# Closing the tile context behind the first three loads, and clearing the semaphores while the last store is under way

## The chip, the cores and the metric

The kernel runs on one core of a Trainium2 chip. A core has five engines that run on their own and meet only through semaphores: PE (matmuls), DVE and ACT (elementwise work and reductions), POOL (here: fills) and SP (here: DMA issues). Sixteen DMA engines move data between HBM and the core's SBUF. The metric is the device time of one execution in microseconds (us). Each kernel is run several times; the median counts.

## The reference

One decode step for two batch entries `b`. Attention over a cache of 32768 positions with 32 query heads on 4 key-value heads, and an MLP mixer on the same `x`, are mixed by a gate:

```python
def reference(A_x, A_k_cache, A_v_cache, A_wq, A_wo, B_x, B_w1, B_w2, B_w3, B_w4, gate_w):
    x = A_x                                            # (2, 1, 1024)
    g = _sigmoid((x * gate_w).sum(-1, keepdims=True))
    q = (x @ A_wq).reshape(2, 1, 32, 128).transpose(0, 2, 1, 3)
    k, v = (jnp.repeat(c, 8, axis=1) for c in (A_k_cache, A_v_cache))   # (2, 4, 32768, 128) each
    p = _softmax(jnp.einsum("bhqd,bhkd->bhqk", q, k) * 128 ** -0.5, axis=-1)
    a = jnp.einsum("bhqk,bhkd->bhqd", p, v).transpose(0, 2, 1, 3).reshape(2, 1, 4096) @ A_wo
    # with one position in the sequence, every shift of the token mixing shifts in zeros: x1 = x
    b = x + _gelu(_layernorm(x) @ B_w3) @ B_w4
    return g * a + (1 - g) * b
```

All arrays are float32. The caches hold 2 x 4 x 32768 x 128 values each, 134 MB, and the kernel reads 331 MB from HBM for an output of 8 KB.

## The kernel before, in words

**Loads.** Two large buffers in SBUF, `load0` and `load1` (the list `ring`, 64 KB in each of 128 partitions), take all large arrays in turn. SP issues every such load through the helper `load` (line 208): it waits until the buffer's last readers are through, then issues the DMA, which adds 16 to a semaphore when it has landed. In order: two halves of `wq` (lines 238 and 239, no wait), two of `w3`, then for each of 8 pairs of batch entry and key-value head two halves of `kt` (the transposed keys) and two of `vt`, with two pieces of `w4` after the fourth pair, and at the end `wo` in four pieces to the ring and four small ones to the buffer `tail`. `xg`, which holds `x` and the gate's weights, is loaded by ACT (line 269, tile `xg_sb`).

**Compute.** While the first loads are in flight, POOL fills the padded operands with zeros (`wide`, `x_pad` to `w_pad`, lines 270 to 276) and DVE makes selection matrices (`sel`, `perm`, lines 279 to 293). When `xg_sb` has landed, DVE and PE make the norm and the gate; PE projects `x` by `wq` (`project`, line 350, matmuls in line 347) and the normed `x` by `w3`. Eight turns follow, one per pair: scores (line 463), exponentials on ACT (line 530), transposes (line 480) and the product with the values (line 489). `weigh` adds the products with `w4` and `wo`. The last pieces of `wo`, in `tail`, are multiplied behind that in two halves (line 370); ACT copies either half out of PSUM (line 612), SP stores the first and ACT the second (line 613).

**Order.** Nothing is scheduled: every engine has a list of instructions in the order of the code, and waits for semaphores that the code counts by hand (`Line.after` is a wait, `Line.take` a wait that also subtracts). All of it stands in one section of the tile framework, `tile_critical` (line 191), whose `sync_engine` is POOL. The framework puts three things around that: a meeting of all engines at the very start (each engine adds to a semaphore behind a drain, POOL waits for four, and releases them); at the section's start a NOP on POOL that the others wait for; at its end a drain on each engine, which POOL gathers, and then, behind ACT's own wait for the two stores (`stored`, line 615), a meeting of all engines, POOL's clear of the semaphores in one instruction, and a second meeting. Instructions of the framework carry the lines 640, 643 and 191 in the profile.

Of the kernel before, what the change touches and what calls it, by code (L numbers as in the profile page):

```python
# [9 lines left out]
F32 = mybir.dt.float32  # L10
# [4 lines left out]
P = 128  # L15
# [4 lines left out]
NI = 4  # L20
# [51 lines left out]
def kernel(  # L72
# [52 lines left out]
    nc = tc.nc  # L125
    scale = DH ** -0.5

    sb = ctx.enter_context(tc.tile_pool(name="sb", bufs=1))
    ps = ctx.enter_context(tc.tile_pool(name="ps", bufs=1, space=bass.MemoryType.PSUM))

    def new(name, *shape, parts=P):
        return sb.tile([parts, *shape], F32, name=name)

    ring = [new(f"load{i}", PART, WIDE) for i in range(2)]
    tail = new("tail", 4 * D)
    xg_sb = new("xg_sb", KD, 3)
    wide = new("wide", 3 * P)
    ones = new("ones", P)
# [38 lines left out]
    f = new("f", REP)  # L177
    so_far = new("so_far", D // G)
    out_sb = [new("out0", P), new("out1", P // 2)]

    sc = [ps.tile([P, 512], F32, name=f"sc{i}") for i in range(NI)]
    tr = [ps.tile([P, 512], F32, name=f"tr{i}") for i in range(2)]
    acc_bank = ps.tile([P, 512], F32, name="acc")
    acc = acc_bank[:, :D // G]
    final = [sc[0][:, :P], sc[1][:, :P // 2]]
    pv = ps.tile([P, 512], F32, name="pv")
    ident = wide[:, P:2 * P]
    compact = ident[:, ::C // B]

    section = ctx.enter_context(ExitStack())  # L190
    section.enter_context(tc.tile_critical(sync_engine=mybir.EngineType.Pool))
    sem = tc.alloc_semaphore
    pe, dve, act, pool = (Line(e, sem(n)) for e, n in (
        (nc.tensor, "pe"), (nc.vector, "dve"), (nc.scalar, "act"), (nc.gpsimd, "pool")))
    sp = Line(nc.sync)
# [1 line left out]
    landed = [sem(f"landed{i}") for i in range(2)]  # L197
    w_in = [*landed, sem("w_in2"), sem("w_in3")]
    got_x = sem("got_x")


    step, own_step, to_pe, pt_in, b_in, e_in, x_in, k1_free = (
        sem(n) for n in ("step", "own_step", "to_pe", "pt_in", "b_in", "e_in", "x_in", "k1_free"))

    came = ((got_x, 32), (b_in, 16), (pt_in, 16), (k1_free, PAIRS + 16))
    stored = x_in

    def load(dst, src, sem, *marks):
        sp.after(*marks)
        nc.sync.dma_start(dst, src).then_inc(sem, 16)  # L210

    def run(src, j):
        return src[PART * j:PART * (j + 1)].rearrange("i (q w) c -> (i q) (w c)", w=PART)

    flat = [t.rearrange("p w c -> p (w c)") for t in ring]
# [7 lines left out]
    def at(name, m=None):  # L223
        if m is None:
            return (pe.sem, 1 + PROLOGUE.index(name))
        return (pe.sem, len(PROLOGUE) + m * len(TURN) + m // 4 * 2 + 1 + TURN.index(name))
# [8 lines left out]

    load(flat[0], run(wq, 0), landed[0])
    load(flat[1], run(wq, 1), landed[1])
    load(flat[0][:, :PART * 2 * F], run(w3, 0), landed[0], at("q0"))  # L240
    load(flat[1][:, :PART * 2 * F], run(w3, 1), landed[1], at("q1"))

# [23 lines left out]
        load(tail[:, 3 * D + i * D // 2:3 * D + (i + 1) * D // 2], run(wo, 1)[:, lo:lo + D // 2], came[2 + i][0])  # L266


    nc.scalar.dma_start(xg_sb, xg).then_inc(got_x, 16)
    pool.mark(nc.gpsimd.memset(wide, 0.0))  # L270
    pool.after((pool.sem, pool.n))
    made = pool.mark(nc.gpsimd.affine_select(
# [325 lines left out]
    for mark, parts in zip(came, (((0, 0), (0, 1), (1, 0), (1, 1)), ((2, 0), (2, 1)), ((3, 0),), ((3, 1),))):  # L598
        pe.after(mark)
        for c, i in parts:  # L600
# [2 lines left out]
                             stop=(c == 3))  # L603
            if c == 3:
                last.then_inc(pe.sem, 1)
    thirty_two = nc.scalar.to_reg(32)

    to = [out.rearrange("(i k b) (h c) -> i h (k b) c", i=2, k=2, h=2)[0],
          out.rearrange("(i k b) (q h c) -> i h (k b q) c", i=2, k=2, q=2, h=2)[1]]
    for i, (line, step_of) in enumerate(((sp, 2 * SHIFT), (act, SHIFT))):  # L610
        act.after(ended(i))
        line.after(act.mark(nc.scalar.copy(out_sb[i], final[i])))  # L612
        line.e.dma_start(to[i], out_sb[i][::step_of]).then_inc(stored, 16)
    section.close()
    nc.scalar.nop(nofuse=True).wait_op(stored, thirty_two, "sem-ge")


# ---- launch: one core; the host only lays the arrays out
# [28 lines left out]
```

## Time and profile before

| | |
|---|---|
| time of the runs, median of 3 | 774.99 us (774.84 to 775.09) |
| span of the profiled execution | 773.0 us |
| PE busy | 434.3 us (56%) |
| DVE, ACT, POOL busy | 94.7, 60.8, 3.6 us |
| mean granted TensorE clock | 0.768 of full speed |
| read from HBM | 331.36 MB, 429 GB/s over the span |

The span of the profiled execution reaches from its first to its last instruction on any engine; the time of a run is longer, since it holds what lies around that. The page lists busy times of the engines without waits, branches, drains and DMA issues; such queue instructions are found by asking for a line of the code, and are marked with a "q" behind the engine's name (SPq, ACTq, POOLq; PEldq is PE's queue). For a DMA issue, the time in the list is that of the issuing instruction, not of the transfer.

### The profile page before, as it was taken

To read this page: it belongs to the slowest core of one execution; us is meant where nothing else is said; L and a number is where in the kernel's file an instruction comes from. 1 tells how busy PE (TensorE), PEld (TensorE's weight loads), DVE (VectorE), ACT (ScalarE), POOL (GpSimd) and SP (SyncE) were. 2 spreads that over 40 slices of the span, in tenths; PEclk is the share of its full clock that TensorE was granted. 3 is DMA by queue.
4 is the path that set the end of the run, shared out by engine and by line. 5 is a ranking of instruction groups with operands and counts; after the bars stand their busy time and mean duration, and the time that the engine had idled before them with its cause. 6 is when DMAs were issued, how large, how long until landed. Compare 5 with 4: busy or idle time off the path is not lost. (4 is left out here: it accounts for less than half of the span.)

```text
span 773.0 us, 7554 instructions
## 1 busy us (share of the span) xinstructions
PE 434.3 (56%) x3380; PEld 196.4 (25%) x3380; DVE 94.7 (12%) x267; ACT 60.8 (8%) x145; POOL 3.6 (0%) x12
## 2 busy tenths in 40 slices
PE   0576746564645474547475446454745465646466
PEld 0232413232322132223233213121312132313133
DVE  1110202100210021002100002100210021002110
ACT  0000002000200020002000002000200020002000
POOL 1000000000000000000000000000000000000000
PEclk9977667767887768766866779777777777779789
DMA  9999999999999999999999999999999999999997
GB/s 380 434 435 435 434 435 435 435 435 434 434 434 434 434 434 431 434 434 434 425 433 435 428 434 434 434 434 434 431 434 434 434 434 434 431 434 434 438 417 313
DMA packets 6805, 331.51 MB, mean 429 GB/s; under 512 B 900, under 2 KB 908, under 8 KB 1292
## 3 DMA queue, kind: packets, MB, share of 16 engines
q1 hardware_dynamic: 6634, 331.36, 99.2%
q8 instruction: 8, 0.13, 0.1%
q10 hardware_dynamic: 162, 0.02, 0.0%
q14 instruction: 1, 0.01, 0.0%
HBM read 331.36 MB, written 0.01 MB: 429 GB/s over the span
## 5 line engine op out<-in xcount | busy, mean ns | idle before, releaser
L463 PE MATMUL sc<-load,q_cur 128*32 128x512 f32 x1024 | 145.0, 727 | 133.1 <-PEq L51 133.1
L489 PE MATMUL pv<-load,pt 128*32 128x512 f32 x1024 | 132.0, 674 | 89.3 <-PEq L51 89.3
L463 PEld LDWEIGHTS sc<-load,q_cur 128*32 128x32 f32 x1024 | 48.0, 131 | 223.9 <-issue 223.0
L489 PEld LDWEIGHTS pv<-load,pt 128*32 128x32 f32 x1024 | 39.0, 123 | 172.3 <-issue 172.3
L480 PE MATMUL sc<-wide,p 128*128 128x128 f32 x256 | 44.4, 347 | 22.8 <-PEq L51 22.8
L546 DVE TENSOR_REDUCE mx<-sc 128x1 f32<-128x512 f32 x32 | 21.4, 689 | 286.4 <-PE sc L463 286.4
L530 ACT ACT_TABLE_LOAD x8 | 10.3, 1283 | 486.0 <-ACTq L51 486.0
L480 PEld LDWEIGHTS sc<-wide,p 128*128 128x128 f32 x256 | 40.0, 184 | 30.0 <-issue 30.0
L361 PE MATMUL acc<-load,w_pad 128*32 128x256 f32 x448 | 33.1, 465 | 18.1 <-PEq L51 18.1
L563 DVE COPY pt<-sc 64x256 f32<-64x256 f32 x64 | 25.9, 415 | 78.4 <-PE sc L480 77.9
L536 ACT COPY pt<-sc 64x256 f32<-64x256 f32 x64 | 23.5, 367 | 82.3 <-PE sc L480 80.0
L568 DVE COPY pv_sb<-pv 128x512 f32<-128x512 f32 x16 | 10.3, 686 | 146.8 <-PE tr L495 146.8
L361 PEld LDWEIGHTS acc<-load,w_pad 128*32 128x32 f32 x448 | 18.1, 133 | 32.4 <-issue 27.0
L499 PE MATMUL tr<-sel,pv_sb 128*128 128x8 f32 x128 | 19.0, 284 | 11.8 <-PEq L51 11.8
L347 PE MATMUL sc<-load,x_pad 128*32 128x512 f32 x128 | 18.6, 746 | 7.0 <-PEq L51 7.0
L499 PEld LDWEIGHTS tr<-sel,pv_sb 128*128 128x128 f32 x128 | 18.5, 230 | 12.3 <-issue 12.3
L530 ACT ACTIVATE p<-sc,bias 128x512 f32<-128x512 f32 x32 | 21.5, 685 | 0.1
L347 PE MATMUL sc<-load,xn_pad 128*32 128x384 f32 (+1 forms) x128 | 15.3, 640 | 7.9 <-PEq L51 7.9
L332 PE MATMUL tr<-xg_sb,perm 128*128 128x16 f32 x4 | 1.0, 372 | 23.1 <-DMA xg_sb<-xg 23.1
L559 DVE COPY p<-p 128x256 f32<-128x256 f32 x32 | 9.4, 294 | 26.7 <-ACT p L530 26.7
L347 PEld LDWEIGHTS sc<-load,x_pad 128*32 128x32 f32 x128 | 4.7, 133 | 20.0 <-issue 20.0
L347 PEld LDWEIGHTS sc<-load,xn_pad 128*32 128x32 f32 x128 | 4.8, 131 | 18.4 <-issue 18.4
(86 smaller groups left out, 96.5 us busy)
## 6 DMA issues: line engine op xcount, KB each, us to landing
load<-w SPq DMA_DIRECT2D x4, 7168.0 KB, 25.3
load<-wo SPq DMA_DIRECT2D x1, 7168.0 KB, 29.0
load<-wo SPq DMA_DIRECT2D x1, 4096.0 KB, 18.1
load<-wo SPq DMA_DIRECT2D x1, 2048.0 KB, 22.6
load<-wo SPq DMA_DIRECT2D x1, 1024.0 KB, 24.6
tail<-wo SPq DMA_DIRECT2D x1, 1024.0 KB, 26.6
tail<-wo SPq DMA_DIRECT2D x1, 512.0 KB, 27.4
tail<-wo SPq DMA_DIRECT2D x2, 256.0 KB, 27.6
```

Source lines behind the costliest of these rows:

```text
L347: last = nc.tensor.matmul(b[C * g:C * g + C, :hi - lo], pad[:, k], t[:, o + lo:o + hi], start=(k == 0), stop=(k == KD - 1))
L361: inst = nc.tensor.matmul(acc[C * g:C * g + C], lhsT, rows[:, g * (D // G):(g + 1) * (D // G)], start=False, stop=last, skip_group_check=True)
L463: last = nc.tensor.matmul(sc[i][C * g:C * g + C], q_cur[:, w, s], ring[j][:, w, o:o + 512], start=(s == 0 and w == 0), stop=(s == 1 and w ...
L480: last = nc.tensor.transpose(sc[k][:, t * P:(t + 1) * P], pair.rearrange("p w q -> p (w q)"), ident)
L489: last = nc.tensor.matmul(pv[C * g:C * g + C], pt[j][w][:, lo:lo + C], ring[j][:, w, o:o + G * DH], start=(j == 0 and w == 0 and t == 0), ...
L499: last = nc.tensor.matmul(tr[1][:, w * REP:(w + 1) * REP], pv_sb[:, s, w].rearrange("p i q -> p (i q)"), sel[:, s], start=(s == 0), stop=( ...
L530: nc.scalar.activation(p[:, i, :, :PART], sc[i].rearrange("p (t q w) -> p t w q", t=NT, w=PART), AF.Exp, bias=bias, scale=scale, accum_out ...
L536: nc.scalar.copy(*halves(1, j, c)).then_inc(pt_in, 1)
L546: last = [nc.vector.reduce_max(out=mx[:, k:k + 1], in_=sc[k], axis=AX.X) for k in ((1, 2) if i == 2 else (i,))][-1]
L559: nc.vector.tensor_copy(p[:, i, :, PART], p[:, i, :, 0]).then_inc(to_pe, 1)
L563: nc.vector.tensor_copy(*halves(0, j, c)).then_inc(pt_in, 1)
L568: last = nc.vector.tensor_copy(pv_sb[:, :, :, i], pv.rearrange("p (s q w) -> p s w q", q=HALF, w=PART))
```

## The change

SBUF and PSUM buffers are taken from the program directly in place of tile pools. The critical section now holds only the first two loads of `wq` and the load of `xg`, its `sync_engine` is SP, and the tile context is closed and compiled right behind it. All instructions after that are written straight to the engines. At the end no framework code is left: SP and ACT each add to a new semaphore `issued` behind their store, POOL waits for both and clears the kernel's semaphores (the list `cleared`, all but `stored`), and ACT's last instruction waits for the stores on `stored`, which has a semaphore of its own now and which ACT itself sets back.

```diff
-    sb = ctx.enter_context(tc.tile_pool(name="sb", bufs=1))
-    ps = ctx.enter_context(tc.tile_pool(name="ps", bufs=1, space=bass.MemoryType.PSUM))
-
     def new(name, *shape, parts=P):
-        return sb.tile([parts, *shape], F32, name=name)
+        return nc.alloc_sbuf_tensor(name, [parts, *shape], F32).ap()
+
+    def bank(name):
+        return nc.alloc_psum_tensor(name, [P, 512], F32).ap()
...
-    section = ctx.enter_context(ExitStack())
-    section.enter_context(tc.tile_critical(sync_engine=mybir.EngineType.Pool))
-    sem = tc.alloc_semaphore
+    cleared = []
+
+    def sem(name):
+        cleared.append(nc.alloc_semaphore(name))
+        return cleared[-1]
+
+    stored = nc.alloc_semaphore("stored")
...
+    issued = sem("issued")
...
-    stored = x_in
...
-    load(flat[0], run(wq, 0), landed[0])
-    load(flat[1], run(wq, 1), landed[1])
+    with tc.tile_critical(sync_engine=mybir.EngineType.SP):
+        for j in range(2):
+            load(flat[j], run(wq, j), landed[j])
+        nc.scalar.dma_start(xg_sb, xg).then_inc(got_x, 16)
+    tc.close()
+    tc.compile()
+
     load(flat[0][:, :PART * 2 * F], run(w3, 0), landed[0], at("q0"))
...
-    nc.scalar.dma_start(xg_sb, xg).then_inc(got_x, 16)
     pool.mark(nc.gpsimd.memset(wide, 0.0))
...
-    thirty_two = nc.scalar.to_reg(32)
...
         line.e.dma_start(to[i], out_sb[i][::step_of]).then_inc(stored, 16)
-    section.close()
-    nc.scalar.nop(nofuse=True).wait_op(stored, thirty_two, "sem-ge")
+        line.e.nop().then_inc(issued, 1)
+    nc.gpsimd.wait_ge(issued, 2)
+    nc.clear_and_free_semaphores(cleared)
+    act.take(stored, 32)
```

The change moves instructions at the two ends of each engine's list. The lists below name an instruction's line in its own kernel, what it writes and reads, and the semaphores that it waits for; plain increments, waits and drains are not listed. The start of SP's list, before (`Pool_sequencer` is the semaphore of POOL's NOP, the barrier is the meeting at the very start):

```order
L643 UNCONDITIONAL_BRANCH [waits barrier_Pool_Activation_PE_DVE_SP_release]
L643 UNCONDITIONAL_BRANCH [waits Pool_sequencer_49]
L210 DMA load_61<-wq 128x16384
L210 DMA load_62<-wq 128x16384
L210 DMA load_61<-w 128x14336 [waits pe]
```

and now:

```order
L652 UNCONDITIONAL_BRANCH [waits barrier_Pool_Activation_PE_DVE_SP_release]
L242 NO_OP
L247 UNCONDITIONAL_BRANCH [waits SP_sequencer_49]
L214 DMA load<-wq 128x16384 x2
L242 UNCONDITIONAL_BRANCH
L242 NO_OP [waits SP_49,SP_sequencer_49,Activation_sequencer_49]
L247 UNCONDITIONAL_BRANCH
L214 DMA load<-w 128x14336 [waits barrier_Pool_Activation_PE_DVE_SP_release,pe]
```

The NOP that lets the first loads go is now SP's own, and between the loads of `wq` and of `w3` stand the section's exit and the meetings of the context's end, which were the last thing in the program.

The end of POOL's list, before:

```order
L276 MEMSET w_pad 128x896
L210 UNCONDITIONAL_BRANCH
L191 UNCONDITIONAL_BRANCH
L191 NO_OP [waits Pool_49,DVE_sequencer_49,PE_sequencer_49,SP_sequencer_49,Activation_sequencer_49,Pool_sequencer_49]
L643 UNCONDITIONAL_BRANCH
L643 ISA [waits barrier_Pool_Activation_PE_DVE_SP_gather]
```

and now, with the context's end ahead of the fills:

```order
L652 UNCONDITIONAL_BRANCH [waits barrier_Pool_Activation_PE_DVE_SP_gather]
L247 UNCONDITIONAL_BRANCH x2
L247 ISA [waits barrier_Pool_Activation_PE_DVE_SP_gather]
L278 MEMSET wide 128x384 [waits barrier_Pool_Activation_PE_DVE_SP_gather]
...
L284 MEMSET w_pad 128x896
L623 ISA [waits issued]
```

The ISA rows are the clears. The one at the end no longer waits for a meeting of all engines, but for SP and ACT alone, and nothing follows it; a second, of the framework's own semaphores, stands near the start between two meetings that POOL, DVE, PE and ACT go through before their first instruction of the set-up.

The end of ACT's list, before:

```order
L612 COPY out_104<-sc_106 128x128 [waits pe]
L612 COPY out_105<-sc_107 128x64 [waits pe]
L613 DMA out<-out_105 2x8x64 [waits act]
L191 UNCONDITIONAL_BRANCH
L643 UNCONDITIONAL_BRANCH [waits Pool_49,x_in]
```

and now:

```order
L619 COPY out<-sc 128x128 [waits pe]
L619 COPY out<-sc 128x64 [waits pe]
L620 DMA out<-out 2x8x64 [waits act]
```

The two branches behind the store are gone; the increment of `issued` and the wait for `stored`, which the list leaves out, follow the store directly.

More of the change, by code (lines that the diff above doesn't have):

```diff
@@ L179 @@
     out_sb = [new("out0", P), new("out1", P // 2)]
-    sc = [ps.tile([P, 512], F32, name=f"sc{i}") for i in range(NI)]
-    tr = [ps.tile([P, 512], F32, name=f"tr{i}") for i in range(2)]
-    acc_bank = ps.tile([P, 512], F32, name="acc")
+    sc = [bank(f"sc{i}") for i in range(NI)]
+    tr = [bank(f"tr{i}") for i in range(2)]
+    acc_bank = bank("acc")
     acc = acc_bank[:, :D // G]
     final = [sc[0][:, :P], sc[1][:, :P // 2]]
-    pv = ps.tile([P, 512], F32, name="pv")
+    pv = bank("pv")
     ident = wide[:, P:2 * P]
     compact = ident[:, ::C // B]
-    section = ctx.enter_context(ExitStack())
-    section.enter_context(tc.tile_critical(sync_engine=mybir.EngineType.Pool))
-    sem = tc.alloc_semaphore
+    cleared = []
[3 more added lines that the diff above has]
+    stored = nc.alloc_semaphore("stored")
     pe, dve, act, pool = (Line(e, sem(n)) for e, n in (
```

## The prediction

> **What bounds the kernel now.** I read the queues and the slices of the span first, then busy times by stretch, then the chain that ended last, and then the queue instructions (drains, semaphore waits, branches) by line at both ends of the program, because that is where the change works.
>
> The page's span, its slice row of DMA, and the queue that carries nearly all bytes:
>
> ```profile
> span 773.0 us, 7554 instructions
> DMA  9999999999999999999999999999999999999997
> q1 hardware_dynamic: 6634, 331.36, 99.2%
> ```
>
> The same by stretch (length, the five engines' busy time, granted clock, DMA share, GB/s):
>
> ```profile
> core 0: us, PE busy (x) PEld busy (x) DVE busy (x) ACT busy (x) POOL busy (x), PEclk, DMA share, GB/s
> 0.00:1.90 1.90, 0.00 (x0) 0.00 (x0) 0.17 (x1) 0.57 (x1) 0.91 (x7) 1.00 0.00 0
> 1.90:38.00 36.10, 10.99 (x72) 4.05 (x72) 5.39 (x20) 2.38 (x4) 2.70 (x7) 1.00 1.03 436
> 38.00:718.00 680.00, 391.46 (x2866) 175.15 (x2866) 83.64 (x227) 55.92 (x135) 0.00 (x0) 0.75 1.00 433
> 741.90:769.60 27.70, 19.38 (x337) 11.44 (x336) 2.11 (x10) 0.10 (x1) 0.00 (x0) 0.82 0.93 391
> 769.60:773.00 3.40, 0.43 (x16) 0.27 (x16) 0.00 (x0) 0.38 (x2) 0.00 (x0) 1.00 0.01 2
> ```
>
> Nothing moves in the first 1.9 us. From there the transfers run at a DMA share of 1.00 with PE idle for over 40% of the long stretch, and nothing but the two stores moves after 769.6. So the time is three pieces in a row: 1.9 us until the first bytes move, 767.7 us of transfers, and 3.4 us behind the last load. An engine's work in the middle counts only if it leaves the queue empty. The last piece, by the chain (start, length) and the timeline:
>
> ```profile
> 741.88 27.71 DMA tail<-wo
> 769.64 0.47 PE sc L370 x16
> ...
> 770.14 0.21 ACT L612 COPY out<-sc 128x64 f32<-128x64 f32 x1 [0.37 <-PE sc L370]
> 770.38 1.10 ACTq L613 DMA_DIRECT2D out<-out  x1
> ```
>
> ACT's store leaves its queue at 770.38 + 1.10 = 771.48. What follows is no tensor work; it stands in the queue instructions of lines 191, 615 and 643 (count, durations in ns, first and last start):
>
> ```profile
> L191 SPq DRAIN  x1: 412/412/412, 770.5 to 770.5; - x1
> L191 ACTq DRAIN  x1: 158/158/158, 771.5 to 771.5; - x1
> L191 POOLq NOP  x1: 13/13/13, 771.8 to 771.8; - x1
> L615 ACTq EVENT_SEMAPHORE  x1: 17/17/17, 772.1 to 772.1; - x1
> L643 POOLq EVENT_SEMAPHORE  x4: 17/17/17, 772.2 to 772.9; - x4
> L643 POOLq DRAIN  x2: 34/64/94, 772.4 to 772.7; - x2
> L643 POOLq EVENT_SEMAPHORE_RANGE_CLEAR  x1: 161/161/161, 772.5 to 772.5; - x1
> L643 PEldq EVENT_SEMAPHORE  x2: 51/51/51, 772.4 to 772.9; - x2
> ```
>
> ACT's wait for the stores is over at 772.1; only then can the five engines meet (772.2 to 772.4), POOL clear the semaphores (772.5), and the engines meet again (772.9). The span ends with PE's last wait, 772.9 + 0.05.
>
> **The change, part by part.**
>
> *The end.* Removed from behind the store's landing: both meetings and the clear. By rows that is 772.95 - (772.1 + 0.017) = 0.83 us; the starts are printed to 0.1 us, so 0.73 to 0.93. In their place ACT waits for `stored` last and ends, at 772.1 as now, since copy, store and landing are the same instructions. The clear moves to POOL behind `issued`. The ACT increment follows its store at 771.48, at about 0.02 us (the 17 ns of an EVENT_SEMAPHORE row). POOL's answer to another engine takes at most 0.1 us here: ACT's drain ended at 771.5 + 0.16 and POOL's NOP started at 771.8. Then a drain of 0.03 to 0.09 and the clear's 0.16: POOL is done by 771.48 + 0.02 + 0.1 + 0.09 + 0.16 = 771.85, 0.27 us ahead of the landing. That landing is the work that hides the clear; without it the end would be POOL's 771.85. The added increment on SP stands behind SP's store alone, which is issued earlier than ACT's, and nothing stands behind it.
>
> *The start.* SP now releases SP and ACT, where POOL did it before. The rows of lines 640, 191 and 643, and the first issues (start, length):
>
> ```profile
> L640 POOLq EVENT_SEMAPHORE  x2: 17/17/17, 0.5 to 0.6; - x2
> L640 SPq EVENT_SEMAPHORE  x1: 17/17/17, 0.7 to 0.7; - x1
> L191 POOLq NOP  x1: 13/13/13, 0.7 to 0.7; - x1
> L643 SPq COMPARE_BRANCH  x1: 33/33/33, 0.7 to 0.7; - x1
> 0.89 0.86 SPq L210 DMA_DIRECT2D load<-wq  x2
> 0.90 0.40 ACTq L269 DMA_DIRECT2D xg_sb<-xg  x1
> ```
>
> POOL's NOP came within 0.1 us of its own release of the engines. SP hears of that release at 0.7, so its NOP starts no earlier than POOL's did, and about 0.05 later if SP takes as long from wait to NOP. From there to the first issue both programs have one semaphore and one branch. I take +0.04 us, with bounds from -0.05 (SP's own semaphore reaches it sooner than POOL's did) to +0.2 (one more branch-to-issue gap, 0.89 - 0.7).
>
> *Between.* Behind the first loads come the section's exit and two meetings with a clear in the middle, for all five engines. SP's loads are out at 0.93 + 0.86 = 1.8. The exit and the meetings that the end shows took from SP's drain (0.41) and then from 771.5 to 773.0, or 1.9 us with the landing still inside. So POOL and DVE begin their set-up at up to 3.7 in place of 0.97 and 1.04, some 2.7 us later. What they feed:
>
> ```profile
> 0.97 0.42 POOL L270 MEMSET wide<- 128x384 f32 x1 [0.53 <-POOLq L191]
> 2.52 2.23 DVE L293 COPY perm<-wide 128x128 f32<-128x128 f32 x2
> 3.76 0.84 POOL L276 MEMSET w_pad<- 128x896 f32 x1
> 23.00 0.18 DVE L300 TENSOR_TENSOR xw<-xg_sb 128x16 f32<-128x16 f32 x1 [18.25 <-DMA xg_sb<-xg]
> 35.33 0.33 SPq L210 DMA_DIRECT2D load<-w  x1
> DMA to landing us min/median/max: 21.9/31.4/40.8
> ```
>
> `perm` was ready at 4.75 and is then ready at 7.5, while the first work on `xg_sb` starts at 23.0: a cover of 15 us. SP's next instruction, the first load of w3, goes out at 35.33 when PE is through with half of wq; the second wq load, issued at 1.35, lands 40.8 us later (the last row is of these two loads), at 42.1. With 1.0 us from issue to first bytes (0.89 to 1.90) the queue would run dry only if that issue came 5.8 us later. Without these covers the 2.7 us would be added to the time; with them the middle costs 0. The tensors keep their places in SBUF and PSUM, and every load its order and size, so the 767.7 us of transfers stay.
>
> *Sum.* 773.0 - 0.83 + 0.04 = 772.2 for the span. The median of the runs, 774.99, lies 2.0 above the span; that part I take as it is. So 774.99 - 0.79 = 774.2, 0.10% below the time before. By the bounds alone (end 0.73 to 0.93, start -0.05 to +0.2) it is 773.9 to 774.5.
>
> The Trainium skill bears on the 2.0 us ("Runtime: NRT & Kernel Launch", The ~15µs preamble/postamble breakdown): behind the kernel the runtime waits for all engines, then each resets about 51 semaphores, at 1.5 us for either and 2 us more. By that page's figures an estimate of 5 us would follow; the measurement leaves 2.0 here and decides on the size. Its order, all engines first and the resets after, would leave this part whole whichever engine is last, against the first rival below.
>
> **The rivals.**
>
> *The part outside the span shrinks too.* If engines do something of their own in the 2.0 us, four of five could now do it while the store is under way. At most four fifths, 1.6 us, would go: 772.6; with half of that, 773.4. For it: PE's last matmuls end at 770.1, so 2 us of its time would be free. Against it: no row shows work there. Chance 0.14, of which 0.11 are below 773.44.
>
> *The drain behind the first loads waits for them* (the slower side). The section's exit drains SP and ACT while 16 MB are in flight. If SP's drain lasted until the loads land at 42.1, all engines would meet at about 43.3 (two meetings of 0.6, after the rows at 772.2 to 772.9), set up until 47.1 (0.97 to 4.75), and need 23.0 to 35.3, 12.3 us more, to free the ring: w3's load goes out at 59.4, its bytes move at 60.4, 18.3 us after the queue ran dry, so 792.5. It starts to cost once the drain ends later than about 24. Against it: ACT's drain behind its store was over at 771.7 and the wait for the landing only at 772.1, so a drain did not wait for a transfer. For it: SP's drain, directly behind a store, took 0.41 us, longer than the others that had nothing to finish. Chance 0.06.
>
> *The clear, or a fetch of instructions, ends last.* If POOL's drain took half a microsecond more, POOL would end at 772.35 and the gain shrink to 0.6: 774.4. The second form is a page of instructions fetched at the end:
>
> ```profile
> q8 instruction: 8, 0.13, 0.1%
> ```
>
> Eight fetches of 16 KB took 0.1% of 16 engines' 773 us, 12 us, or 1.5 us each. The order of blocks has changed, so one could fall on ACT's last instructions: 774.2 + 1.5 = 775.7. The Trainium skill (same page, Instruction fetch mechanics) says that a taken branch to a page outside the window waits for such a fetch. That speaks against the branches that the change adds at the head, and would make the time 775.7 too if SP met one; in the trace SP's branch at 0.7 is followed by the issue at 0.89, with no fetch between, so the trace shows no such wait at this place. Chance 0.08.
>
> **How the numbers follow.** The forecast has 0.72, with its own range 773.8 to 774.6. The predicted time is 774.2. The range of 8 in 10 runs from 773.2, which takes in a third of the first rival, to 775.2, which takes in most of the last: 0.72 + 0.05 + 0.06 = 0.83. Faster or slower by over 0.2% (1.55 us, about what a measurement of this kernel tells from no change) means below 773.44 or above 776.54. Faster: 0.11, from the first rival. Slower: 0.06 from the drain and 0.01 from the last, 0.07. Within: 0.82.
>
> **What would show it.** In the changed kernel's profile: SP's first issue at 0.9 to 1.0; the clear on POOL starting at 771.6 to 771.8 and over before ACT's last wait; that wait, at about 772.15, the last instruction of the span; a span near 772.2; no meeting behind it. In the middle: w3's first load still at 35 to 36 and no slice of DMA below 9 before the last. If POOL's set-up starts far beyond 4 us, the drain rival is right in kind; if w3's load goes out after 41, also in price. If the span is 772.2 but the time below 773.4, the first rival is right. A clear that starts behind 772.1 would be the last. If the transfers themselves take more or less than 767.7 us by over half a microsecond, none of these mechanisms has it, and the prediction is wrong for a reason that I have not named.

## The result, and the profile after

| | before | after |
|---|---|---|
| time, median of 21 runs | 774.94 us (774.67 to 775.14) | 773.90 us (773.70 to 774.19) |
| span of the profiled execution | 773.0 us | 772.3 us |
| median time less that span | 1.9 us | 1.6 us |

The ratio of the times is 0.9986, with an interval of 0.9980 to 0.9993: 1.04 us faster, 0.13%, where 0.8 us was forecast. Of that, 0.7 us lies in the span of the profiled execution and 0.3 us behind it. The spans are printed to 0.1 us. The stretches of the kernel after, with the columns shown before (length, five engines' busy time, granted clock, DMA share, GB/s):

```profile
span 772.3 us, 7548 instructions
DMA  9999999999999999999999999999999999999997
...
0.00:2.00 2.00, 0.00 (x0) 0.00 (x0) 0.00 (x0) 0.00 (x0) 0.20 (x4) 1.00 0.00 1
2.00:38.00 36.00, 11.53 (x72) 4.44 (x72) 5.55 (x21) 2.94 (x4) 3.40 (x8) 0.96 1.03 437
38.00:718.00 680.00, 387.93 (x2866) 176.67 (x2866) 83.61 (x227) 55.91 (x135) 0.00 (x0) 0.75 1.00 433
...
742.00:769.70 27.70, 19.04 (x341) 11.88 (x340) 2.11 (x10) 0.08 (x1) 0.00 (x0) 0.88 0.93 391
769.70:772.30 2.60, 0.43 (x16) 0.27 (x16) 0.00 (x0) 0.40 (x2) 0.00 (x0) 0.96 0.01 3
```

The first bytes move at 2.0 instead of 1.9 and the transfers take as long as they did: 0.1 us later at either end. In this pair of profiles all of the span's gain is in the last row, 2.6 us in place of 3.4. Its end, by the timeline and the queue rows of the lines that clear (623) and wait (51, the helper `take`):

```profile
770.26 0.21 ACT L619 COPY out<-sc 128x64 f32<-128x64 f32 x1 [0.37 <-PE sc L378]
770.50 1.11 ACTq L620 DMA_DIRECT2D out<-out  x1
L621 ACTq EVENT_SEMAPHORE  x1: 17/17/17, 771.6 to 771.6; - x1
L623 POOLq DRAIN  x1: 82/82/82, 771.7 to 771.7; - x1
L623 POOLq EVENT_SEMAPHORE_RANGE_CLEAR  x1: 132/132/132, 771.8 to 771.8; - x1
L51 ACTq EVENT_SEMAPHORE  x1: 17/17/17, 772.2 to 772.2; - x1
```

ACT reports its store at 771.6, POOL's clear starts at 771.8 and is over 0.13 later; ACT's wait for the stores at 772.2 is the last instruction. At the start, the first issues, POOL's first fill, the first work on `xg_sb` and SP's first load of w3:

```profile
0.92 0.41 ACTq L245 DMA_DIRECT2D xg_sb<-xg  x1
0.96 0.88 SPq L214 DMA_DIRECT2D load<-wq  x2
2.91 0.42 POOL L278 MEMSET wide<- 128x384 f32 x1 [2.47 <-POOLq L247]
13.26 0.17 DVE L308 TENSOR_TENSOR xw<-xg_sb 128x16 f32<-128x16 f32 x1 [6.57 <-DMA xg_sb<-xg]
23.00 9.53 PE L355 MATMUL sc<-load,x_pad 128*32 128x512 f32 x64 [6.48 <-PEq L51]
32.59 0.33 SPq L214 DMA_DIRECT2D load<-w  x1
```

SP's first load is 0.07 later than before and now behind ACT's load of `xg`, and the first work on `xg` starts ten microseconds earlier (13.3 against 23.0). The drains of the section's exit, with both loads of wq in flight, took next to nothing:

```profile
L242 ACTq DRAIN  x1: 8/8/8, 1.9 to 1.9; - x1
L242 SPq DRAIN  x1: 55/55/55, 2.0 to 2.0; - x1
```

### The profile page after: what moved, and what is told of

Same layout as the page of the kernel before. It is cut to its first block, busy times and chain, and to the rows that moved or that the text cites. A ratio compares the mean times of both kernels' runs of the same rounds, so it can differ in the third digit from the quotient of the medians.

```text
span 772.3 us, 7548 instructions
## 1 busy us (share of the span) xinstructions
PE 431.1 (56%) x3380; PEld 198.3 (26%) x3380; DVE 94.6 (12%) x267; ACT 60.8 (8%) x145; POOL 3.6 (0%) x12
## 5 line engine op out<-in xcount | busy, mean ns | idle before, releaser
L471 PE MATMUL sc<-load,q_cur 128*32 128x512 f32 x1024 | 146.9, 734 | 133.0 <-PEq L51 133.0
L471 PEld LDWEIGHTS sc<-load,q_cur 128*32 128x32 f32 x1024 | 52.7, 132 | 221.1 <-issue 219.3
L369 PE MATMUL acc<-load,w_pad 128*32 128x256 f32 x448 | 29.9, 428 | 19.6 <-PEq L51 19.6
L355 PE MATMUL sc<-load,xn_pad 128*32 128x384 f32 (+1 forms) x128 | 17.4, 711 | 9.3 <-PEq L51 9.3
## 6 DMA issues: line engine op xcount, KB each, us to landing
load<-wo SPq DMA_DIRECT2D x1, 2048.0 KB, 22.1
```

The costliest lines, as they stand in the source:

```text
L355: last = nc.tensor.matmul(b[C * g:C * g + C, :hi - lo], pad[:, k], t[:, o + lo:o + hi], start=(k == 0), stop=(k == KD - 1))
L369: inst = nc.tensor.matmul(acc[C * g:C * g + C], lhsT, rows[:, g * (D // G):(g + 1) * (D // G)], start=False, stop=last, skip_group_check=True)
L471: last = nc.tensor.matmul(sc[i][C * g:C * g + C], q_cur[:, w, s], ring[j][:, w, o:o + 512], start=(s == 0 and w == 0), stop=(s == 1 and w ...
```

## The experiments

All kernels below start from the changed kernel; each was run 11 times (the one with 120 meetings once), in three sets, each on another chip. The first and the last hold the changed kernel itself again, the second does not; the kernel before ran in all three and took 774.87, 774.89 and 774.87 us, so they compare. Where a mean span or a mean of what lies outside it is given, it is over the 11 runs, from the span that each run lists (to 0.1 us) and its time.

**The changed kernel again**, in the first set and in the last.

> The changed kernel as it is, for comparison within this set. Every theory: span 772.3, time 773.9 (773.7 to 774.1).

> The changed kernel once more, for comparison within this set: 773.85.

It took 773.84 us in both. The kernel before took 774.87 beside it. By means over both sets its span is 772.33 against 773.08 before, and the part outside 1.54 against 1.82: 0.75 and 0.28 us of gain.

**The old end put back.**

```diff
     nc.gpsimd.wait_ge(issued, 2)
-    nc.clear_and_free_semaphores(cleared)
     act.take(stored, 32)
+    nc.all_engine_barrier()
+    nc.clear_and_free_semaphores(cleared)
+    nc.all_engine_barrier()
```

> The changed kernel, with the end as it was before: ACT waits for the stores, all engines meet, POOL clears, all engines meet again. Theory A (the gain is made at the end alone, in two parts: 0.8 us of span, and about 0.3 us that the runtime behind the span waits for PE and POOL, which react later to their own end than ACT): span 773.1, time 775.0, slightly above the kernel before because the first load starts 0.07 later. Theory B (what follows the span is shorter for another reason, such as that the framework's code no longer stands at the end of the program): span 773.1, time 774.7. Theory C (part of the gain is made in the middle or at the start): time 774.5 or less.

774.91 us, the time of the kernel before (ratio 1.0001, 0.9992 to 1.0010), with a mean span of 773.07 and 1.85 outside. Against the changed kernel of this set (772.30 and 1.57 by means) that is 0.77 us of span and 0.29 outside. So the end alone makes the gain, both parts of it: theory C falls, and B with its unchanged part outside. Where the span goes is read from the rows of the second meeting (line 626):

```profile
L626 POOLq EVENT_SEMAPHORE  x2: 17/17/17, 772.9 to 772.9; - x2
...
L626 PEldq EVENT_SEMAPHORE  x1: 51/51/51, 773.0 to 773.0; - x1
```

**The clear behind the landing, without meetings.**

```diff
     nc.gpsimd.wait_ge(issued, 2)
-    nc.clear_and_free_semaphores(cleared)
-    act.take(stored, 32)
+    nc.gpsimd.wait_ge(stored, 32)
+    nc.clear_and_free_semaphores([*cleared, stored])
```

> The changed kernel, with POOL waiting for the stores itself and clearing behind that; ACT ends behind its store. The clear is no longer hidden, but there is still no meeting. POOL's drain and clear took 0.08 + 0.03 + 0.13 us, so the span is 772.5 (0.25 more). Theory A (POOL reaches the runtime's meeting some 0.5 us behind its last instruction, where ACT takes 0.15): time 774.45, 0.55 above the control. Theory B (what follows the span is the same whichever engine ends last): time 774.15, 0.25 above the control.

774.42 us, 0.58 above the control: theory A had 774.45, B 774.15. Against the control of this set the mean span rose by 0.29 to 772.59, and the part outside by 0.31 to 1.88. So half of that cost does not show in the span at all: it arises where POOL's last instruction is late.

```profile
L624 POOLq DRAIN  x1: 88/88/88, 772.7 to 772.7; - x1
L624 POOLq EVENT_SEMAPHORE_RANGE_CLEAR  x1: 134/134/134, 772.8 to 772.8; - x1
```

These two rows, with the gaps around them, are the 0.29 us (the profiled execution itself ended 0.4 us later than the mean, at 773.0, for reasons ahead of its store).

**The last wait on another engine.** One kernel replaces `act.take(stored, 32)` by `pe.take(stored, 32)`, another by `sp.take(stored, 32)`.

> The changed kernel, with the last wait for the stores on PE instead of ACT; ACT ends behind its store. The span grows by 0.03 to 0.05 (PE's wait row is 51 ns, ACT's 17). Theory A (PE reaches the runtime's meeting 0.33 us behind its last instruction, where ACT takes 0.15): time 0.2 above the control, 774.1. Theory B (the same whichever engine ends last): 773.95.

> The changed kernel, with the last wait for the stores on SP instead of ACT. Theory A (the runtime's meeting is passed from PE to ACT, POOL, DVE and SP; POOL's arrival, some 0.5 us behind its clear, is nearly as late as ACT's): POOL's arrival now sets it, and the time falls by no more than 0.05 us against the control, 773.85. Theory B (only the last instruction of the span counts): the same time as the control, 773.9. Rival: SP, in whose queue the wait comes at no cost, saves the whole way of the meeting from ACT to SP, 0.13 us: 773.77.

PE: 773.90 us, 0.06 above the control by medians and 0.10 by means (standard error 0.06), 0.08 of it outside the span. Theory A had 0.2 and B 0.05: A is too large for PE, and times alone do not tell more. SP: 773.81, 0.03 below by medians and 0.07 by means, with the part outside unchanged (1.53 against 1.54). That fits A and B; the 0.13 of the rival did not come.

What separates the readings is a semaphore that is not the kernel's. No instruction of the kernel names number 2, yet it is updated eighteen times ahead of the kernel's first instruction and eighteen times behind its last, the latter in two rows of nine. I take it for the runtime's, the software that starts and ends the kernel. The trace's record of the first five updates behind the kernel (us from the span's start), and the end of the span:

```
kernel                  1st      2nd      3rd      4th      5th      end of span
before                773.294  773.328  773.437  773.481  773.505    772.964
after                 770.398  772.400  772.458  772.503  772.526    772.255
old end put back      773.269  773.303  773.517  773.561  773.584    773.035
clear late            770.807  772.285  773.507  773.550  773.574    772.968
last wait on PE       772.620  772.654  772.693  772.736  772.759    772.381
last wait on SP       770.429  771.907  772.489  772.532  772.555    772.286
combined (below)      770.383  771.948  771.987  772.031  772.455    772.322
```

The runs tell whose updates these are. With the last wait on PE the 1st moves from 770.4 to 772.6; with ACT released from the wait, the 2nd comes at 771.9; with the late clear only the 3rd waits, so it is POOL's; with SP's wait last and an early clear, the 5th. Each comes no earlier than the one before it plus 0.02 to 0.05 us: a meeting in which each engine waits for the one ahead. In it POOL is slow. Its update came 0.54 us after the end of its clear in both kernels where only POOL held the row up (773.507 against the clear's end at 772.97, and 772.489 against 771.95 with the wait on SP). Behind a semaphore instruction, which ended at 772.876, it took 0.56 in the kernel before. ACT took 0.15 behind its last wait (772.400 against 772.255), 0.23 behind an increment (771.907 against 771.680, with the wait on SP) and 0.28 behind its store (771.948 against 771.672 in the combined kernel); PE took 0.24 (772.620 against 772.381; 0.33 in the kernel before), SP 0.13 (772.455 against 772.322). Why POOL takes longer, no run here shows.

So what lies outside the span depends on which engine is last. Before, POOL held the row, but only by 0.07: 773.437 against 773.367, which PE's update of 773.294 alone would have made (with the last wait on PE, the 3rd comes 0.073 after the 1st). The second meeting ended late on both, and both had to go. The 3rd update stood 0.47 behind the end of the span before and stands 0.20 behind it after, 0.27 less. After, POOL's 772.458 is 0.02 later than ACT's 772.400 asks for (0.04 from the 2nd to the 3rd in the combined kernel).

The last of the eighteen updates moves with the end of what is timed: in the 13 profiled executions of the changed kernel and of its variants, it stands 0.11 to 0.12 us beyond the time of that execution. Between the two rows of nine lie 0.78 to 0.80 us in ten of the 14 profiles and 0.88 to 0.89 in four, whichever kernel it is. So single executions differ by 0.1 us outside the span for a reason that no experiment here touches.

**POOL in place of SP as the releasing engine.**

```diff
-    with tc.tile_critical(sync_engine=mybir.EngineType.SP):
+    with tc.tile_critical(sync_engine=mybir.EngineType.Pool):
```

> The changed kernel, with POOL instead of SP as the section's releasing engine, as it was before. Theory S (SP's own NOP costs 0.07 us at the first load, and the landing of xg does not matter): SP's first load goes out at 0.89 instead of 0.96, xg is issued behind it and lands near 23 us again instead of 13, the first load of w3 goes out near 35 instead of 32.6, and the time is 0.05 to 0.1 below the control, 773.8. Rival X (the earlier landing of xg is worth something): the time is the control's or above it, 773.9 to 774.2.

> The kernel with POOL as the releasing engine, once more, since its first runs left open whether 0.07 us at the first load reach the end. If they do: 0.07 to 0.1 below this set's control. If the end of the transfers does not follow their start by so little: as the control within 0.05.

The first issues are those of the kernel before again:

```profile
0.89 0.86 SPq L214 DMA_DIRECT2D load<-wq  x2
35.43 0.33 SPq L214 DMA_DIRECT2D load<-w  x1
...
DMA to landing us min/median/max: 22.1/22.1/22.1
```

The last row is of `xg`, which landed 22.1 us after its issue, at 23 us, and w3 was 2.8 us later than with SP releasing. The time was 773.85 and 773.75 against 773.84 in either control; over all 22 runs a side, the mean is 0.04 us lower with a standard error of 0.04. Rival X falls: ten microseconds of `xg` are worth nothing. Whether the 0.07 us of the first issue reach the end stays open; both 0 and 0.1 are within two standard errors.

**More waiting in the middle.** 40 and 120 further meetings of all engines behind `tc.compile()`.

```diff
     tc.compile()
+    for _ in range(40):
+        nc.all_engine_barrier()
```

> The changed kernel with 40 more meetings of all engines behind the tile context, at about 0.3 us each: 12 us of added waiting before the set-up. Theory of the prediction (the middle is covered by the transfers): POOL's first fill at about 14.5 instead of 2.9, the first work on xg at about 18 instead of 13.3, PE's projection still near 23 and the first load of w3 near 32.6; time as the control, 773.9 within 0.15. Rival (each meeting costs its length): 785.

> 120 added meetings behind the tile context. The 40 moved POOL's first fill from 2.91 to 17.46, or 0.364 us each, and the first load of w3 went out 16.4 us behind that fill. With 120: fill at 46.6, w3's first load at 63.0, its bytes from 64.0, while the wq loads are through at 42.1. Theory of the prediction (only what lasts longer than the transfers in flight costs): 21.9 us of empty queue and 795.8 us in all. Rival (the added waiting counts in full once it shows): 817. Rival (there is more cover than the first two loads): below 790.

The 40 cost nothing: 773.83 us, with POOL's first fill 14.6 us later and PE's projection 1.4 us later.

```profile
17.46 0.42 POOL L280 MEMSET wide<- 128x384 f32 x1 [17.02 <-POOLq L249]
24.42 9.40 PE L357 MATMUL sc<-load,x_pad 128*32 128x512 f32 x64
```

The 120 cost 22.6 us (796.42 us, one execution). Fill, first load of w3, and the stretch in between:

```profile
45.81 0.42 POOL L280 MEMSET wide<- 128x384 f32 x1 [45.37 <-POOLq L249]
61.38 0.33 SPq L214 DMA_DIRECT2D load<-w  x1
...
2.00:42.00 40.00, 0.00 (x0) 0.00 (x0) 0.00 (x0) 0.00 (x0) 0.00 (x0) 1.00 0.99 420
42.00:64.00 22.00, 14.13 (x100) 5.07 (x104) 4.45 (x21) 2.94 (x4) 3.56 (x8) 1.00 0.12 40
64.00:740.00 676.00, 389.06 (x2834) 166.15 (x2830) 83.66 (x227) 55.98 (x135) 0.00 (x0) 0.76 1.00 433
```

The transfers are full until 42.0. In the row of 22 us behind that the DMA share is 0.12, all of it at the row's two ends: by the trace's packets w3's first bytes move at 62.3, 0.96 us after its issue, and from 42.0 to 62.3 the share is 0.01. So the cover is what the prediction took it for, the first two loads, and it ends at 42 us. w3's load went out 1.6 us earlier than expected, with which the same arithmetic gives 20.3 us; the time lost was 22.6, so about 2 us of the loss are not in that sum, and why stays open. The rivals, 817 and below 790, fall.

**A kernel that ends sooner.** SP and ACT report to POOL ahead of issuing their store, and SP has the last wait; once with POOL releasing the first loads, once with SP.

```diff
         line.after(act.mark(nc.scalar.copy(out_sb[i], final[i])))
+        line.e.nop().then_inc(issued, 1)
         line.e.dma_start(to[i], out_sb[i][::step_of]).then_inc(stored, 16)
-        line.e.nop().then_inc(issued, 1)
     nc.gpsimd.wait_ge(issued, 2)
     nc.clear_and_free_semaphores(cleared)
-    act.take(stored, 32)
+    sp.take(stored, 32)
```

> Both ideas together and one more: POOL releases the first loads, SP has the last wait, and ACT and SP report their store to POOL ahead of issuing it, so that POOL clears about a microsecond earlier. ACT's increment stands ahead of its store and delays it by about 0.05 us. Theory A: 0.07 to 0.1 from the start, 0.13 from the meeting, less 0.05: time 773.75 (0.15 below the control). Theory B: start's 0.07 less 0.05: 773.9.

> The changed kernel with SP's last wait and the reports ahead of the stores, but with SP still releasing the first loads. If the gain of the combined kernel is made at the end (POOL clears a microsecond earlier, SP's slot in the runtime's meeting is the last): as the combined kernel, 773.64, or 0.2 below this set's control. If 0.1 of it came from POOL's earlier release: 773.74.

773.64 us with POOL releasing (ratio to the kernel before 0.9984, 0.9975 to 0.9993) and 773.70 with SP. Both beat the changed kernel's 773.84, by 0.20 and 0.14 (by means 0.21 and 0.17, standard error 0.03). The first gained more than theory A had (773.75); the second lies between its two expectations, 773.64 and 773.74, so what the release by POOL adds stays open here too. POOL now clears at 770.6, before ACT's store is issued:

```profile
770.24 0.21 ACT L619 COPY out<-sc 128x64 f32<-128x64 f32 x1 [0.37 <-PE sc L378]
770.57 1.11 ACTq L621 DMA_DIRECT2D out<-out  x1
L623 POOLq EVENT_SEMAPHORE_RANGE_CLEAR  x1: 132/132/132, 770.6 to 770.6; - x1
```

The report does delay ACT's store: from the copy's end to the issue 0.12 us, against 0.03 in the changed kernel. The mean span is the control's all the same (772.30 with POOL releasing, 772.35 with SP, 772.33 for the control); the part outside fell from 1.54 to 1.36 and 1.34, since POOL no longer holds up the runtime's meeting (3rd update at 771.987 in the list above) and SP's update, the last on the way, follows its own wait. It takes both. With SP's wait alone, POOL held the row at 772.489 and nothing was gained outside the span. The early clear alone was not run; by the steps of the row, an estimate, ACT's wait would then hold it and 0.02 be gained.

## Why the prediction was right

*What bounds the kernel* held: 1.9 to 2.0 us until the first bytes, the transfers, and the end. The transfers kept their length; the one part that shrank is the end, and putting the old end back returned the old time.

*The end* was sized at 0.83 us of span (0.73 to 0.93). The spans differ by 0.7 in the profiled executions and by 0.75 in the mean; put back alone, the old end costs 0.77 us of span. The chain came step by step as written: report, drain, clear, 0.3 us ahead of the landing's wait. The value of hiding the clear is shown by the late clear: 0.58 us.

*The start* was put at +0.04 us; the first issue is +0.07 (0.96 against 0.89), inside the bounds. What it costs at the end could not be measured.

*The middle at nothing* was right, with the cover named and its edge measured at 42 us. POOL's set-up began at 2.91, within the "up to 3.7". One sign in it was wrong: w3's first load was to go out at 35 to 36 and went out at 32.6, because `xg` went ahead of SP's load into the DMA queues: its first bytes moved at 1.97, ahead of wq's at 2.01, where in the kernel before they moved at 5.0, behind wq's at 1.9. That made the cover larger and the time no different.

*The part outside the span* is the step that failed in size. It was taken as unchanged at 2.0 us; by means it was 1.82 and fell by 0.28. The first rival named the place, but its mechanism, engines doing work of their own there, sized it at 0.8 to 1.6. What the runs show is smaller and more exact: each engine reaches the runtime's meeting some time after its own last instruction, POOL 0.54 to 0.57 us, PE 0.24 to 0.33, ACT 0.15 behind its wait, and the change took the late instructions of POOL and PE away. With that term, 774.94 - 0.75 - 0.28 = 773.91, against 773.90 measured. The Trainium skill ("Runtime: NRT & Kernel Launch", The ~15µs preamble/postamble breakdown) puts a wait for all engines ahead of the runtime's resets, and was used against that rival. The order agrees with the trace: behind the first six of the nine updates, from 773.62 to 774.29 in the kernel before, 249 other semaphores are each updated once. That this wait costs the same whichever engine is last was my conclusion from it, and the late clear's 0.31 us outside the span contradicts it.

The bounds of the sum were added up wrongly: 774.99 - 0.93 - 0.05 is 774.0 and not 773.9. So the measured 773.90 lies below all that the named terms allow. That it lies inside the range down to 773.2 is owed to the room left for the first rival, which had the place right and the mechanism wrong; the forecast's own range reached 773.8 without a term for it, which is luck.

*The drain that waits for the loads* is refuted: SP's and ACT's drains behind 16 MB in flight took 55 and 8 ns. Its price was put too high as well: the rows from 772.2 to 772.9 hold both meetings and the clear, 0.8 us where the sum took 1.2. *A late clear* did not occur: it was over before the landing. *A fetch at the end* did occur, in both kernels, and cost nothing that shows: by the trace's packets 16 KB moved on the instruction queue from 769.4 to 770.9 before and from 769.5 to 770.7 after, over before ACT's report at 771.6, and nothing moved on it behind that. The eight fetches took 1.06 us each in the kernel before; the 1.5 us of the prediction came from a share printed as 0.1%.

## What to carry to other kernels

A kernel that fills its DMA queues from start to end still has what stands behind the last store: meetings and clears there cost their full length, and can go under the store's own flight. When moving them, look at which engine's last instruction is late, not only at the end of the span: an engine that is slow into the runtime's closing, here POOL, should finish first. Waiting that is placed behind the first loads was free up to the moment when the next load had to be issued, and cost at least its whole length from there: 20.3 us of empty queue cost 22.6, in one execution.

## What was not expected of the hardware

POOL takes 0.53 to 0.57 us from its last instruction to the runtime's first meeting behind the kernel, where SP takes 0.13, ACT 0.15 to 0.28 and PE 0.24 to 0.33. That late arrival, with PE's, is why the time fell by more than the span did; POOL's alone made 0.07 us of it, because PE's stood right behind, and 0.31 where POOL was last by itself (the late clear).

When a small load landed went with the order of two issues within 0.04 us. With ACT's issue of `xg` (12 KB) at 0.92 and SP's first large load at 0.96, `xg` landed 12.2 to 12.6 us after its issue, in all ten profiles; with SP's at 0.89 and ACT's at 0.90, 22.1 to 22.4 us, in all four. Neither changed the time of the kernel by more than the error.
